# Placing a slot's products with v behind the last quarter of feed-forward products, in a one-core threshold attention and feed-forward kernel

## The chip, the cores and the metric

The kernel runs on one core of one Trainium2 chip. The metric is device microseconds of one launch, the median of several runs. In the profile PE is TensorE (matmul), PEld its weight loads, DVE is VectorE, ACT is ScalarE, POOL is GpSimd and SP is SyncE, which here issues nearly all DMA transfers.

## The reference, cut to what matters

There are 8 batches of 8 heads with 576 tokens and 64 features per head, all in float32. Each score row keeps only what lies within `tau` of its maximum; the attention output, with the heads side by side, is the 576 x 512 input `x` of a feed-forward block with a residual.

```python
scores = scale * np.matmul(q, k.transpose(0, 1, 3, 2))
thresh = np.max(scores, axis=-1, keepdims=True) - tau
scores = np.where(scores >= thresh, scores, -1000000000.0)
attn = np.exp(scores - np.max(scores, axis=-1, keepdims=True))
attn = attn / (np.sum(attn, axis=-1, keepdims=True) + 1e-09)
x = np.matmul(attn, v)                      # then (B, S, H*D)
...
xn = (x - mu) / np.sqrt(var + 1e-06) * g_ln
return x + np.maximum(xn @ w_ch1, 0.0) @ w_ch2
```

## The kernel before, in words

**Slots.** The attention of a batch is cut into 9 slots, s = 0 to 8 (`SLOTS`, L63), so there are 72 slots n = 9b + s (`NS`), all counted from 0. In slots 0 to 3 a pair of heads has its first 256 query rows treated, in slots 5 to 8 its second 256 rows; slot 4 (`s == HP`) takes the last 64 rows of all 8 heads. `scores` (L367) writes a slot's scores into two accumulator tiles, `sc[0]` and `sc[1]`, one for each head of the pair. Each has 1536 columns (three banks of 512): 128 free ones, and then two blocks of 576 columns (L354 to L358). The scores of a head go out in four pieces, and the pieces of both heads are given in turn. The last 256 columns of `sc[0]`, behind its scores, are called `pv_behind` (L356).

**Weights of the attention.** `exponentials` (L390) takes the row maxima (DVE, L398) and the exponentials (ACT, L409). `weights` (L411) masks them with the threshold and sums them (DVE, L416), and takes the reciprocal `den` (L420). The weights must then stand with the keys along the partitions. In batch 0 TensorE turns them, by products with diagonal matrices of `1/den` (`turn_weights`, L443), and ACT copies them out. The diagonals are made on ACT (L427), in batch 0 alone. From batch 1 on (`blocks_go`), POOL divides (L429), DVE transposes 32 x 32 blocks (`turn_blocks`, L494), and the result goes to DRAM and comes back as `em` and `rest` through SP's queue (`fetch`, L505). `em` has one buffer.

**Products with v.** `values_of` (L520) multiplies `v` with the turned weights of the slot before: 20 matmul records for a slot (80 shorter ones for slot s = 4). They go to `pv_behind`, except in batch 0 up to s = 4, where they go to a small tile of the pool `ps_ff`. ACT copies them into `x` (L555; for s = 4 two copies, L546), and POOL adds them to the sum for the mean (L564).

**Feed-forward.** The 576 rows of a batch make two groups of 288 tokens. `ffn_steps` (L632) is a generator over one group: for each of 16 parts of the hidden layer an accumulation `p1` of 4 products, copied out by ACT with a relu (L649), then for each of 4 output parts an accumulation `p2` of 16 products, taken out by DVE (L596). A product is two matmuls, four records (`product`, L95). `p1`, `p2`, `mean`, `var` and the turned weights share two buffers of `ps_ff` (tag `ff`).

**The order.** Every engine gets its instructions in the order in which the program gives them (`manual_schedule`, L136). A slot gives its scores, and then four quarters of feed-forward steps, `second_part(n, 0)` to `second_part(n, 3)` (L702). How many steps a quarter gets follows from fixed shares (`ROOM`, L681) and from when the next group is ready (`ready`, L695). Around the quarters calls are run that were put down for a later slot and quarter with `at_quarter` (L688) by `run(n, i)` (L691). The products with v of slot n are put down for slot n + 1, quarter 3 (quarter 1 in batch 0 up to s = 4). `run(n, 3)` stands ahead of `second_part(n, 3)`, so the order on TensorE is: scores, quarters 0, 1, 2, products with v, quarter 3, scores of the next slot. In the first dozen slots `tick` gives pieces of a conversion of the weights `w_ch1` and `w_ch2` from 64-bit numbers to DVE, ACT and POOL as well.

Of the kernel before, what the change touches and what calls it, by code (L numbers as in the profile page):

```python
# [8 lines left out]
F32 = mybir.dt.float32  # L9
# [9 lines left out]
def kernel(  # L19
# [31 lines left out]
    nc = tc.nc  # L51
# [4 lines left out]
    HP = H // 2  # L56
# [4 lines left out]
    TOK = S // 2  # L61
    QH = 256
    SLOTS = 2 * HP + 1  # L63
    NG = 2 * B
    NS = B * SLOTS
# [8 lines left out]
    ffn = ctx.enter_context(tc.tile_pool(name="ffn", bufs=2))  # L74
# [8 lines left out]
    ident = consts.tile([128, 128], F32, name="ident")  # L83
# [18 lines left out]
    def load_qk(u, engines=(nc.sync, nc.sync), room=None):  # L102


        b, hp = units[u]
        tiles = []
        for i, (name, src) in enumerate((("q", q), ("k", k))):
            if room is None:
                t = ins.tile([128, NB, 32], F32, tag=name, bufs=1, name=f"{name}_in")
            else:  # L110
                t = room[:, i * S : i * S + S].rearrange("p (n c) -> p n c", c=32)
            for h in range(2):
                for e in range(2):
                    g = 2 * h + e
                    engines[i].dma_start(  # L115
                        out=t[32 * g : 32 * g + 32],
                        in_=src[b, 2 * hp + h, :, 32 * e : 32 * e + 32].rearrange(
                            "(n r) c -> r n c", r=32
                        ),
                    )  # L120
            tiles.append(t)
        loaded[u] = tuple(tiles)
# [43 lines left out]
    class Weights:  # L166
# [139 lines left out]
        def tick(self):  # L306
            self.ticks += 1
            if self.ended < self.masked:
                self.end()
            if self.masked < self.carried and self.due[self.masked] <= self.ticks:  # L310
                self.mask()
            if self.carried < self.begun:
                self.carry()
            if self.begun < self.fetched:
                self.begin()
# [51 lines left out]
    def scores(b, s):  # L367


        hp, half = (s, 0) if s < HP else (s - HP - 1, 1)  # L370

        pieces = []
        for h in range(2):
            t = 0
            for j in range(2):
                first = FREE + j * S
                for at, n in span(first, S):
                    pieces.append((t, h, j, at, n, at - first))
                    t += n
        for t, h, j, at, n, o in sorted(pieces):  # L380
            r = slice(64 * h, 64 * h + 64)
            for i in range(2 if s == HP else 1):
                qT, kT, ql = turned[b * HP + (2 * j + i if s == HP else hp)]
                nc.tensor.matmul(  # L384
                    sc[h][64 * i : 64 * i + 64 if s == HP else 128, at : at + n],
                    lhsT=ql[r] if s == HP else qT[r, half, j * 128 : (j + 1) * 128],
                    rhs=kT[r, o : o + n], start=True, stop=True,
                )

    def exponentials():  # L390


        neg = small.tile([128, 4], F32, tag="neg", name="neg")
        thr = small.tile([128, 4], F32, tag="thr", name="thr")
        es = att.tile([128, 4, S], F32, tag="e", name="e")
        for h in range(2):
            i = slice(2 * h, 2 * h + 2)
            nc.vector.tensor_reduce(  # L398
                out=neg[:, i], in_=pairs[h],
                axis=AXL.X, op=ALU.max, negate=True,  # L400
            )
            nc.gpsimd.tensor_scalar(  # L402
                out=thr[:, i], in0=neg[:, i], scalar1=-1.0, scalar2=low_sb,
                op0=ALU.mult, op1=ALU.add,
            )
        for i in range(4):
            if i == 2:
                yield es, thr
            nc.scalar.activation(es[:, i], blocks[i], func=AF.Exp, bias=neg[:, i : i + 1])  # L409

    def weights(es, thr, divide):  # L411


        den = small.tile([128, 4], F32, tag="den", name="den")
        for i in range(4):
            nc.vector.scalar_tensor_tensor(  # L416
                out=es[:, i], in0=blocks[i], scalar=thr[:, i : i + 1], in1=es[:, i],
                op0=ALU.is_ge, op1=ALU.mult, accum_out=den[:, i : i + 1],
            )
        nc.vector.reciprocal(den, den)  # L420
        diags = []
        for i in range(4):
            if not divide:
                if i % 2 == 0:
                    two = ffn.tile([128, TOK], F32, tag="o", bufs=6, name="diag")
                diags.append(two[:, i % 2 * 128 : i % 2 * 128 + 128])
                nc.scalar.mul(diags[i], ident, den[:, i : i + 1])  # L427
                continue
            nc.gpsimd.tensor_scalar(  # L429
                out=es[:, i], in0=es[:, i], scalar1=den[:, i : i + 1], scalar2=1.0,  # L430
                op0=ALU.mult, op1=ALU.mult,
            )
        return diags


# [152 lines left out]
    def run_all(calls):  # L588
        now = calls[:]
        calls.clear()  # L590
        for fn in now:
            fn()
# [86 lines left out]
    QUARTERS = 4  # L679
# [11 lines left out]
    def run(n, i):  # L691
        for fn, args in later_calls.pop((n, i), ()):
            fn(*args)

    def ready(g):  # L695

        if g < 2:
            return (24, 42)[g]
        b, t = divmod(g, 2)
        return QUARTERS * (b * SLOTS + (HP, 2 * HP)[t] + 2) + (2, 4)[t]  # L700

    def second_part(n, i):  # L702

        nonlocal issued, owed
        if not queue:
            return
        at = QUARTERS * n + i
        g = issued // STEPS
        left = sum(ROOM[t % QUARTERS] for t in range(at, ready(g + 1))) if g + 1 < NG else 0
        owed += ((g + 1) * STEPS - issued) * ROOM[i] / left if left > 0 else 8  # L710


        got = 1 if i == 0 else 2
        while queue and (owed >= 0.5 or got == 1 and i in (0, QUARTERS - 1)):
            got = next(queue[0], None)
            if got is None:
                queue.pop(0)
                got = 1
            elif got == 0:
                owed = 0.0  # L720
                break
            else:
                issued += 1
                owed -= 1
# [24 lines left out]
    for n in range(NS):  # L749
        b, s = divmod(n, SLOTS)  # L750
        ticks = (1, 3, 4)[: 2 + n // 3] if n < 6 else range(1, 7)

        def tick(i):
            if i in ticks:
                conversion.tick()

        scores(b, s)
        run(n, -1)
        rest = exponentials()
        es, thr = next(rest)  # L760
        run(n, 0)
        conversion.fetch(2)
        run_all(stores)
        second_part(n, 0)
        next(rest, None)

        u = (n + 1) // SLOTS * HP + (n + 1) % SLOTS
        if (n + 1) % SLOTS < HP and u < len(units):
            turn(u)
            if u + 1 < len(units):  # L770
                load_qk(u + 1)
        run_all(aside)
        tick(1)
        run(n, 1)
        second_part(n, 1)
        tick(2)
        blocks_go = by_blocks(b * HP)
        diags = weights(es, thr, blocks_go)
        run_all(aside)
        run_all(stores)  # L780
        tick(3)
        run(n, 2)
        second_part(n, 2)
        tick(4)
        box = []
        if blocks_go:
            scr = turn_blocks(s, es)
            at_quarter(n + 1, 0, lambda s=s, scr=scr, box=box: box.append(fetch(s, scr)))
        else:
            made = turn_weights(s, es, diags)  # L790
            at_quarter(n + 1, -1, next, made)
            at_quarter(
                n + 1, 0 if s <= HP else -1, lambda made=made, box=box: box.append(next(made))
            )
        at_quarter(
            n + 1, 1 if b == 0 and s <= HP else 3,
            lambda b=b, s=s, box=box: values_of(b, s, box[0]),
        )
        if s in (HP, 2 * HP):
            group_ready(2 * b + (s > HP))  # L800
        run_all(aside)
        conversion.fetch(2)
        tick(5)
        run(n, 3)
        if b == 0 and s < HP - 2:
            load_v(s + 2)
        elif n >= SLOTS - 2 and (n + 2) % SLOTS < HP and n < NS - 2:
            load_v((n + 2) // SLOTS * HP + (n + 2) % SLOTS)
        second_part(n, 3)
        tick(6)  # L810
        run_all(aside)
    while later_calls or queue or aside or stores:
# [36 lines left out]
```

## Time and profile before

| | |
|---|---|
| time before, median of 3 | 1444.91 us (1443.7 to 1446.37) |
| profiled span | 1443.0 us |
| TensorE busy | 1389.0 us (96%) |
| VectorE, ScalarE, GpSimd busy | 60%, 29%, 30% |
| feed-forward matmuls, `p1` and `p2` | 515.2 and 513.7 us |
| scores, a slot's 16 matmul records | about 2.2 us |
| products with v, a slot's 20 matmul records | about 2.4 us |
| copy of these products into x (ACT, L555) | 373 ns |

Busy time of a matmul is from its start to its modelled end; neighbours overlap, so busy sums are no throughput. An idle time is put down to the engine whose release came last. A slot from batch 1 on lasts some 17 to 21 us.

### The profile page before, as it was taken

To read this page: it belongs to the slowest core of one execution; us is meant where nothing else is said; L and a number is where in the kernel's file an instruction comes from. 1 tells how busy PE (TensorE), PEld (TensorE's weight loads), DVE (VectorE), ACT (ScalarE), POOL (GpSimd) and SP (SyncE) were. 2 spreads that over 40 slices of the span, in tenths; PEclk is the share of its full clock that TensorE was granted. 3 is DMA by queue.
4 is the path that set the end of the run, shared out by engine and by line. 5 is a ranking of instruction groups with operands and counts; after the bars stand their busy time and mean duration, and the time that the engine had idled before them with its cause. 6 is when DMAs were issued, how large, how long until landed. Compare 5 with 4: busy or idle time off the path is not lost.

```text
span 1443.0 us, 29649 instructions
## 1 busy us (share of the span) xinstructions
PE 1389.0 (96%) x12168; PEld 859.7 (60%) x12168; DVE 871.8 (60%) x1492; ACT 422.2 (29%) x818; POOL 439.1 (30%) x681
## 2 busy tenths in 40 slices
PE   5879999999999999999999999999999999999998
PEld 3655666655556565655556555565556555565664
DVE  5998857556565666566655565556665566656111
ACT  3887513132221313132221312223132322213020
POOL 2444332333323233232322333232332323222100
PEclk8999999999999999999999999999999999999999
DMA  9622466657845677557855577555775578555301
GB/s 226 168 73 83 90 137 157 172 148 162 176 133 145 148 173 173 145 131 171 183 150 145 146 160 167 140 144 143 176 167 143 136 170 185 139 144 137 79 6 17
DMA packets 466840, 205.12 MB, mean 142 GB/s; under 512 B 275024, under 2 KB 428368, under 8 KB 466704
## 3 DMA queue, kind: packets, MB, share of 16 engines
q1 hardware_dynamic: 461936, 202.64, 58.4%
q8 instruction: 95, 1.56, 0.5%
q10 hardware_dynamic: 4736, 0.59, 0.4%
q14 instruction: 41, 0.34, 0.1%
q0 software_dynamic: 32, 0.00, 0.0%
HBM read 119.41 MB, written 83.76 MB: 141 GB/s over the span
## 4 chain that ended last, share of the span: by engine, by line
PE 85%; DVE 4%; DMA 4%; SPq 3%; ACT 2%; issue 1%; POOL 0%; POOLq 0%; DVEq 0%; ACTq 0%
PE p L100 64%; PE sc L538 10%; PE sc L384 9%; SPq L115 2%; DMA em<-scr 1%; DVE e L416 1%; PE tp L100 1%; DVE neg L398 1%; DMA v_in<-in_v_dram 1%; ACT e L409 1%; DMA rest<-scr 0%; DMA scr<-et 0%; PE mean L100 0%; DVE w L263 0%; SPq L500 0%
## 5 line engine op out<-in xcount | busy, mean ns | idle before, releaser
L100 PE MATMUL p<-xc,w 128*64 128x288 f32 x4096 | 515.2, 407 | 7.4 <-ACT hidden L649 5.9
L100 PE MATMUL p<-hidden,w 128*64 128x288 f32 x4096 | 513.7, 407 | 0.0
L100 PEld LDWEIGHTS p<-xc,w 128*64 128x64 f32 x4096 | 294.9, 137 | 211.9 <-ACT hidden L649 12.6
L100 PEld LDWEIGHTS p<-hidden,w 128*64 128x64 f32 x4096 | 297.9, 137 | 196.5 <-issue 9.3
L398 DVE TENSOR_REDUCE neg<-sc 128x2 f32<-128x1152 f32 x144 | 188.7, 1352 | 252.2 <-PE sc L384 252.2
L409 ACT ACTIVATE e<-sc,neg 128x576 f32<-128x576 f32 x288 | 194.5, 742 | 296.5 <-DVE neg L398 290.1
L429 POOL TENSOR_SCALAR e<-e,den 128x576 f32<-128x576 f32 x252 | 187.9, 763 | 239.6 <-DVE den L420 239.5
L416 DVE SCALAR_TENSOR_TENSOR e<-sc,thr,e 128x576 f32<-128x576 f32 x288 | 219.0, 810 | 23.7 <-ACT e L409 23.7
L494 DVE STREAM_TRANSPOSE et<-e 128x1152 f32<-128x1152 f32 x112 | 153.6, 1375 | 77.3 <-POOL e L429 57.1
L649 ACT ACTIVATE hidden<-p 128x288 f32<-128x288 f32 x256 | 105.7, 413 | 292.0 <-PE p L100 290.6
L384 PE MATMUL sc<-kT,qT 64*128 64x384 f32 (+3 forms) x1024 | 150.6, 425 | 20.0 <-DVE qT L344 10.0
L402 POOL TENSOR_SCALAR thr<-neg,low_sb 128x2 f32<-128x2 f32 x144 | 41.6, 289 | 387.4 <-DVE neg L398 382.5
L384 PEld LDWEIGHTS sc<-kT,qT 64*128 64x128 f32 x1024 | 94.2, 191 | 77.5 <-issue 27.0
L538 PE MATMUL sc<-em,v_in 128*64 128x256 f32 (+1 forms) x1408 | 131.3, 330 | 6.0 <-DMA em<-scr 2.2
L538 PEld LDWEIGHTS sc<-em,v_in 128*64 128x64 f32 x1408 | 86.9, 137 | 45.8 <-DVE et L494 7.0
L555 ACT COPY x<-sc 128x256 f32<-128x256 f32 x60 | 22.4, 373 | 286.4 <-PE sc L538 284.4
L596 DVE TENSOR_TENSOR o<-p,rb 128x288 f32<-128x288 f32 x64 | 28.4, 443 | 127.9 <-PE p L100 127.9
L597 POOL TENSOR_TENSOR o<-o,x 128x288 f32<-128x288 f32 x64 | 51.0, 797 | 115.4 <-DVE o L596 114.0
L564 POOL TENSOR_TENSOR sum<-sum,x 128x256 f32<-128x256 f32 (+1 forms) x64 | 32.8, 512 | 97.6 <-ACT x L555 95.1
L655 POOL TENSOR_TENSOR sq<-sq 128x288 f32<-128x288 f32 x48 | 38.8, 808 | 44.0 <-ACT sq L653 41.5
L538 PE MATMUL sc<-rest,v_rest 128*64 128x256 f32 (+1 forms) x352 | 44.7, 329 | 0.0
L100 PE MATMUL tp<-diag,e 128*64 128x128 f32 x576 | 35.5, 278 | 6.6 <-ACT em L462 5.3
(130 smaller groups left out, 701.2 us busy)
## 6 DMA issues: line engine op xcount, KB each, us to landing
scr<-et SPq DMA_DIRECT2D x252, 288.0 KB, 4.6
em<-scr SPq DMA_DIRECT2D x63, 1024.0 KB, 5.9
out_dram<-ot SPq DMA_DIRECT2D x256, 36.0 KB, 4.4
q_in<-in_q_dram SPq DMA_DIRECT2D x124, 72.0 KB, 3.8
k_in<-in_k_dram SPq DMA_DIRECT2D x120, 72.0 KB, 2.8
v_in<-in_v_dram SPq DMA_DIRECT2D x64, 128.0 KB, 4.4
rest<-scr SPq DMA_DIRECT2D x63, 128.0 KB, 6.0
w<-in_moe_w_ch_dram SPq DMA_DIRECT2D x10, 512.0 KB, 6.0
```

What stands on the lines that cost most here:

```text
L100: nc.tensor.matmul(out[r], lhsT=lhsT[:, r], rhs=rhs, **flags)
L384: nc.tensor.matmul(sc[h][64 * i : 64 * i + 64 if s == HP else 128, at : at + n], lhsT=ql[r] if s == HP else qT[r, half, j * 128 : (j + 1) ...
L398: nc.vector.tensor_reduce(out=neg[:, i], in_=pairs[h], axis=AXL.X, op=ALU.max, negate=True,)
L402: nc.gpsimd.tensor_scalar(out=thr[:, i], in0=neg[:, i], scalar1=-1.0, scalar2=low_sb, op0=ALU.mult, op1=ALU.add,)
L409: nc.scalar.activation(es[:, i], blocks[i], func=AF.Exp, bias=neg[:, i : i + 1])
L416: nc.vector.scalar_tensor_tensor(out=es[:, i], in0=blocks[i], scalar=thr[:, i : i + 1], in1=es[:, i], op0=ALU.is_ge, op1=ALU.mult, accum_o ...
L429: nc.gpsimd.tensor_scalar(out=es[:, i], in0=es[:, i], scalar1=den[:, i : i + 1], scalar2=1.0, op0=ALU.mult, op1=ALU.mult,)
L494: nc.vector.transpose(et[:, :, 64 * h : 64 * h + 64].rearrange("p n (j c) -> p j n c", j=2), es[:, 2 * h : 2 * h + 2].rearrange("p j (n c) ...
L538: nc.tensor.matmul(dst[64 * h : 64 * h + 64], lhsT=vt[:, c, h, :] if c < J else vr[:, h, :], rhs=pick(em[:, c] if c < J else er, hp, h), s ...
L597: nc.gpsimd.tensor_tensor(out=o, in0=o, in1=groups[g][:, m], op=ALU.add)
L649: nc.scalar.activation(hidden[:, d], p1, func=AF.Relu)
L655: nc.gpsimd.tensor_tensor(out=sq[:, 0], in0=sq[:, 0], in1=sq[:, c], op=ALU.add)
```

## The change

The function `weights` no longer makes the diagonals; a function `diagonals` does. Up to s = 4 of batch 0 it is called at once, as before. In slots 5 to 8 it is called behind quarter 2's products, so that on ACT the relu copies of that quarter go ahead of the diagonals.

From batch 1 on (`blocks_go`), the products with v of slot n are put down for a quarter 4 of slot n + 1, which `run(n, QUARTERS)` runs behind `second_part(n, 3)`. The order on TensorE becomes: scores, quarters 0, 1, 2, 3, products with v, scores of the next slot. The purpose is to give the way through DRAM (`turn_blocks`, `fetch`) a quarter's products more time before its data are wanted. This holds for the slots n = 9 to 70; the last slot's products stay in quarter 3.

```diff
-        diags = []
-        for i in range(4):
-            if not divide:
-                if i % 2 == 0:
-                    two = ffn.tile([128, TOK], F32, tag="o", bufs=6, name="diag")
-                diags.append(two[:, i % 2 * 128 : i % 2 * 128 + 128])
-                nc.scalar.mul(diags[i], ident, den[:, i : i + 1])
-                continue
+        for i in range(4 if divide else 0):
             nc.gpsimd.tensor_scalar(
...
+        return den
+
+    def diagonals(den):
+        diags = []
+        for i in range(4):
+            if i % 2 == 0:
+                two = ffn.tile([128, TOK], F32, tag="o", bufs=6, name="diag")
+            diags.append(two[:, i % 2 * 128 : i % 2 * 128 + 128])
+            nc.scalar.mul(diags[i], ident, den[:, i : i + 1])
         return diags
...
-        diags = weights(es, thr, blocks_go)
+        den = weights(es, thr, blocks_go)
+        if n <= HP:
+            diags = diagonals(den)
...
         run(n, 2)
         second_part(n, 2)
+        if HP < n < SLOTS:
+            diags = diagonals(den)
...
         at_quarter(
-            n + 1, 1 if b == 0 and s <= HP else 3,
+            n + 1, QUARTERS if blocks_go and n + 1 < NS else 1 if b == 0 and s <= HP else 3,
             lambda b=b, s=s, box=box: values_of(b, s, box[0]),
         )
...
         second_part(n, 3)
+        run(n, QUARTERS)
         tick(6)
         run_all(aside)
```

## The prediction, made before the result

> **What bounds the kernel now.** I read the page first, parts 1 and 4.
>
> ```profile
> PE 1389.0 (96%) x12168; PEld 859.7 (60%) x12168; DVE 871.8 (60%) x1492; ACT 422.2 (29%) x818; POOL 439.1 (30%) x681
> ...
> PE 85%; DVE 4%; DMA 4%; SPq 3%; ACT 2%; issue 1%; POOL 0%; POOLq 0%; DVEq 0%; ACTq 0%
> ```
>
> TensorE is busy for 96%, and 85% of the chain that ended last is on it. So the time is TensorE's work plus its idle time, and an edit is worth what it adds to or takes from that idle time. Next, the waits of TensorE alone, from 191 us (the start of slot 10) to the end, where the products with v are moved:
>
> ```profile
> PE sc L538 <- DMA em<-scr: 2.2, 3, 1.3
> PE p L100 <- ACT hidden L649: 2.1, 3, 0.7
> PE sc L538 <- DVE sq L624: 1.9, 1, 1.9
> PE sc L538 <- DVE et L494: 1.0, 1, 1.0
> PE sc L538 <- issue: 0.8, 1, 0.8
> PE p L100 <- DVE o L596: 0.7, 1, 0.7
> ```
>
> The columns are the total in us, how often, and the longest. The four rows of L538 are the wait that the change aims at: 5.9 us in 6 of 62 slots. The other rows, 2.8 us, belong to feed-forward products. There is little to win: 8.7 us in all.
>
> Then the timeline of one slot's end (slot 18), which the change rearranges:
>
> ```profile
> 347.73 1.90 PE L538 MATMUL sc<-em,v_in 128*64 128x256 f32 x16
> ...
> 349.46 0.60 PE L538 MATMUL sc<-rest,v_rest 128*64 128x256 f32 x4
> ...
> 349.89 2.60 PE L100 MATMUL p<-hidden,w 128*64 128x288 f32 x20
> 350.11 0.37 ACT L555 COPY x<-sc 128x256 f32<-128x256 f32 x1 [9.81 <-PE sc L538]
> ...
> 352.41 1.81 PEld L384 LDWEIGHTS sc<-kT,qT 64*128 64x128 f32 x16 [0.44 <-issue]
> 352.41 2.21 PE L384 MATMUL sc<-kT,qT 64*128 64x384 f32 x16
> ```
>
> ACT copies the products out of `sc[0]` 0.05 us after their end, while TensorE is at quarter 3; the next scores come 1.9 us after that copy. The reader should ask: what if those scores stood directly behind the products with v? They write the same tile, `sc[0]`. So, last, how finely is this tile guarded? Batch 0, where scores come close behind the masks, shows it:
>
> ```profile
> 71.93 0.81 DVE L416 SCALAR_TENSOR_TENSOR e<-sc,thr,e 128x576 f32<-128x576 f32 x1
> 72.67 0.07 DVE L416 DVE_READ_ACCUMULATOR e<-sc,thr,e 128x1 f32 x1
> ...
> 72.80 0.91 PE L384 MATMUL sc<-kT,qT 64*128 64x384 f32 x2 [0.40 <-DVE e L416]
> ...
> 74.15 0.07 DVE L416 DVE_READ_ACCUMULATOR e<-sc,thr,e 128x1 f32 x1
> ...
> 74.27 2.20 PE L384 MATMUL sc<-kT,qT 64*128 64x384 f32 x14 [0.56 <-DVE e L416]
> ```
>
> The first piece of head 0 (columns 128 to 511 of `sc[0]`) starts only when the second mask, which reads columns 704 to 1279, is done at 72.74; head 1's starts when the fourth is done, at 74.22. Neither column nor bank overlaps, and yet the piece waits: the guard is on the whole tile.
>
> The records of the weight loads say the same about ACT. From slot 8 on, the first load of a slot's scores carries a wait on ACT's semaphore in 62 of 64 slots. It is missing in slots 12 and 21, and these are the slots before which a `p1` of quarter 3 had itself to wait for a relu given behind the copy. In slots 0 to 5, whose products go to another tile, none has it. So the first scores of a slot already wait for the copy L555; in the kernel before it is long done.
>
> **What the Trainium skill says.** "PSUM — Partial Sum Buffer", section "PSUM bank collisions raise a hardware error": TensorE and ScalarE must not touch one bank and quadrant at once, so such pairs have to be ordered. `pv_behind` shares its bank with the last piece of `sc[0]`, so some wait is needed; the trace shows it at the first piece, which is in another bank. The same page, "Engine vs sequencer instructions": matmuls start and complete in program order. The trace agrees: at 72.80 the other head's piece waits behind. "Perfetto Trace Analysis", "Identifying Dependency Chains": find an engine's gaps and then the semaphore waited for; that is how I read the records here.
>
> **The change part by part.**
>
> Products with v last. The same instructions run; two effects follow.
>
> (a) Their data get one more quarter, 5 to 9 steps of four records, each record about 0.124 us (92 in 11.38 us): 2.5 to 4.5 us. The longest wait is 1.9 us, so all six go. A wait also costs the overlap of neighbouring matmuls: one lasts 0.406 us and the next pair would start 0.24 us after its start, so 0.17 us each. Gain: 5.9 + 6 x 0.17 = 6.9 us. `em` is released later, but its transfer is issued 1.6 us or more after the scores start, when the products will have ended.
>
> (b) The copy moves between the products' end and the next scores, and nothing is queued on TensorE that may pass it: quarter 0 stands behind the scores. Worked out on slot 18: the last pair of products starts at 349.67, the next would start 0.215 later, and a change from such matmuls to scores costs some 0.10 more (last feed-forward start 352.07, pair 0.24, scores 352.41): 349.98 without a wait. With it: end 350.05, ACT 0.06 later (0.045 to 0.073 over the slots), copy 0.373, ACT to TensorE 0.05 (a copy of `em` from 167.90, 0.59 long; TensorE at 168.54): 350.54. So 0.55 us for each. Behind s = 4 there are two copies (0.27 each, the second 0.16 after the first): 0.61. Scores follow moved products 61 times (slots 11 to 71), 7 of them behind s = 4: 54 x 0.55 + 7 x 0.61 = 34.0 us. ACT is free then: its last relu of quarter 3 is given 2.2 us earlier. Behind the copy ACT has the exponentials, which wait for the new scores' maxima anyway; POOL's adds are wanted only a quarter or more later.
>
> I bound (b) by 0.45 (copy, with latencies half hidden) and 0.80 (0.49 idle plus the full lost overlap of 0.27): 27 to 49 us.
>
> (c) Quarter 3 directly behind quarter 2: could its accumulations wait for buffers? `p2` accumulations end in quarters 1 and 3 there, not in 2, so DVE, busy with the block transposes, holds none up; a relu takes 0.41 us against 2 us of the accumulation between. Nothing.
>
> Diagonals. They last 1.28 us for four on ACT. In slot 6 TensorE waits 2.76 us at 111.73 for two relus at 111.27, which stand behind the diagonals at 108.39; with these behind them the wait shrinks by 1.3 us. In slot 7 the two relus at 135.52 cost TensorE nothing, in slot 8 quarter 2 has no relu, and in slot 5 no feed-forward runs; there the first turning products want the diagonals a little sooner than they come, at most some 0.3 us. I take a gain of 1.3, and between -0.5 and 2.8.
>
> Sum: 34.0 - 6.9 - 1.3 = 25.8 us more: 1444.9 + 25.8 = 1470.7.
>
> **The rivals.** First, the guard is by bank: then only the last piece of `sc[0]`, 1.6 us behind the first, waits for the copy, which is done 0.5 us after the products; nothing is lost and the gains stay: 1444.9 - 8.2 = 1436.7, faster. For it speaks that a bank is all that has to be guarded; against it speak the start at 72.80 and the place of the waits in the records. I give it 5%. Second, stall and gains are as said, but the copy is regularly held up on ACT, or the first scores behind a stall fill the array anew, so that a slot loses 0.80: 49 - 8 = 41 more, 1486. For it: matmuls behind an idle spell start slower (the first score matmul lasts 0.587 us against 0.482); against it: they do so already behind feed-forward products. 12%. Third, stall and gains cancel, 1444.9: the stall would have to be 0.13 us, less than the copy alone. 2%.
>
> **How the numbers follow.** The forecast has 81%, the rivals 5, 12 and 2%. The range takes the lower bound of the stall with the full gains (27 - 8, 1464, and a little less) and reaches to the second rival's edge: 1462 to 1484; what lies below is the first and third rival, above half of the second. Faster 0.05, within 0.2% 0.02, slower 0.93.
>
> **What would show it.** In the profile of after TensorE's waits get a new row at its top: scores L384 waiting for the copy L555 (ACT `x`), some 54 times about 0.48 us, and L546 7 times, about 29 us of idle in all; the rows of L538 waiting for `em` are gone; TensorE's share falls to some 94 to 95%; at 111 us the wait is near 1.5 us. I am wrong if scores start at once behind the products, if idle time before L384 is under 15 us, or if new waits stand before quarter 3's `p`.

## The result, and the profile after

The changed kernel takes 1470.87 us (median of 6 runs, 1469.79 to 1472.86) against 1444.11 us before in the same session: a ratio of 1.0186, 95% interval 1.0173 to 1.0199. It is slower by 26.8 us; 25.8 were forecast.

In the page of after, parts 1 and 4, TensorE has the same 12168 matmuls, a smaller share of a longer span, and ScalarE's share of the chain that ended last rises from 2% to 4%:

```profile
PE 1392.2 (95%) x12168; PEld 854.9 (58%) x12168; DVE 867.4 (59%) x1492; ACT 421.2 (29%) x818; POOL 437.2 (30%) x681
...
PE 87%; DVE 6%; ACT 4%; issue 1%; DMA 0%; POOL 0%; POOLq 0%; ACTq 0%; DVEq 0%
```

The DMA share of the chain fell from 4% to under half a per cent. What took its place stands in TensorE's waits of after, from 191 us to the end (total, how often, longest, in us):

```profile
PE sc L384 <- ACT x L558: 26.6, 54, 0.6
PE sc L384 <- ACT x L549: 3.7, 7, 0.5
PE p L100 <- ACT hidden L652: 2.1, 3, 0.7
PE p L100 <- DVE o L599: 0.7, 1, 0.7
```

The rows of the products with v (L538 before, L541 now) have vanished, and with them 5.9 us of idle time. Two new rows hold 30.3 us: the scores of 61 slots wait for the copy of the products, 54 times for the one copy (L558, L555 before) and 7 times for the two of slot s = 4 (L549). The last two rows are those of before, to a tenth. The end of slot 18 in after's timeline:

```profile
353.28 1.90 PE L541 MATMUL sc<-em,v_in 128*64 128x256 f32 x16
...
355.00 0.60 PE L541 MATMUL sc<-rest,v_rest 128*64 128x256 f32 x4
355.65 0.37 ACT L558 COPY x<-sc 128x256 f32<-128x256 f32 x1 [12.24 <-PE sc L541]
356.07 1.81 PEld L384 LDWEIGHTS sc<-kT,qT 64*128 64x128 f32 x16 [0.93 <-ACT x L558]
356.08 2.21 PE L384 MATMUL sc<-kT,qT 64*128 64x384 f32 x16 [0.47 <-ACT x L558]
```

Products end at 355.60, the copy runs from 355.65 to 356.02, the scores start at 356.08. Each step follows the one before within 0.06 us, and TensorE has nothing to do beside them. From the start of slot 18's scores to that of slot 19's it is 19.06 us now (337.02 to 356.08) and was 18.51 (333.90 to 352.41).

### The profile page after: what moved, and what is told of

The parts are those of the page before. It is cut to its first block, busy times and chain, and to the rows that moved or that the text cites. A ratio compares the mean times of both kernels' runs of the same rounds, so it can differ in the third digit from the quotient of the medians.

```text
span 1469.6 us, 29637 instructions
## 1 busy us (share of the span) xinstructions
PE 1392.2 (95%) x12168; PEld 854.9 (58%) x12168; DVE 867.4 (59%) x1492; ACT 421.2 (29%) x818; POOL 437.2 (30%) x681
## 4 chain that ended last, share of the span: by engine, by line
PE 87%; DVE 6%; ACT 4%; issue 1%; DMA 0%; POOL 0%; POOLq 0%; ACTq 0%; DVEq 0%
PE p L100 65%; PE sc L384 10%; PE sc L541 10%; ACT x L558 1%; DVE neg L398 1%; DVE e L416 1%; ACT e L409 1%; PE tp L100 1%; DVE w L263 1%; DVE w L290 1%; PE mean L100 0%; PE var L100 0%; DMA et<-in_moe_w_ch_dram 0%; DVE w L267 0%; DVE stage L267 0%
## 5 line engine op out<-in xcount | busy, mean ns | idle before, releaser
L100 PEld LDWEIGHTS p<-xc,w 128*64 128x64 f32 x4096 | 291.2, 137 | 217.2 <-ACT hidden L652 14.2
L541 PE MATMUL sc<-em,v_in 128*64 128x256 f32 (+1 forms) x1408 | 130.7, 329 | 0.0
L558 ACT COPY x<-sc 128x256 f32<-128x256 f32 x60 | 22.3, 372 | 330.0 <-PE sc L541 330.0
L541 PEld LDWEIGHTS sc<-em,v_in 128*64 128x64 f32 x1408 | 85.6, 137 | 38.8 <-issue 0.4
L567 POOL TENSOR_TENSOR sum<-x 128x256 f32<-128x256 f32 (+1 forms) x32 | 16.8, 524 | 145.0 <-ACT x L558 89.0
L541 PE MATMUL sc<-rest,v_rest 128*64 128x256 f32 (+1 forms) x352 | 44.3, 329 | 0.0
```

Of the source, the lines that this page charges most:

```text
L100: nc.tensor.matmul(out[r], lhsT=lhsT[:, r], rhs=rhs, **flags)
L541: nc.tensor.matmul(dst[64 * h : 64 * h + 64], lhsT=vt[:, c, h, :] if c < J else vr[:, h, :], rhs=pick(em[:, c] if c < J else er, hp, h), s ...
L567: nc.gpsimd.tensor_tensor(out=sums[g][:, cols], in0=x[:, 0, cols] if c == 1 else sums[g][:, cols], in1=x[:, c, cols], op=ALU.add,)
```

## The experiments

Times are medians; the kernel before took 1444.73 us beside the first four and 1444.90 us beside the last three.

**The diagonals alone.** Against the changed kernel:

```diff
-            n + 1, QUARTERS if blocks_go and n + 1 < NS else 1 if b == 0 and s <= HP else 3,
+            n + 1, 1 if b == 0 and s <= HP else 3,
```

> The diagonals moved as in the change, the products with v left in quarter 3. My theory: the change's gain from the diagonals is the shorter wait in slot 6 (2.8 to 1.6 us) and a little in slot 6's turning, less 0.6 lost in slot 9: about 1.2 us less than before, 1442.9 us; the waits of L538 for em stay near 6 us. Rival, that ACT's load in batch 0 only shifts the wait to a later slot: 1444.1, no change.

Measured: 1441.32 us, ratio 0.9979 (0.9970 to 0.9988), so faster by 3.0 us, with 1.7 to 4.3 as the interval. In its timeline of slot 6 the two relus now stand ahead of the diagonals:

```profile
109.15 0.72 ACT L652 ACTIVATE hidden<-p 128x288 f32<-128x288 f32 x2
...
109.63 1.68 PE L100 MATMUL p<-xc,w 128*64 128x288 f32 x12 [1.60 <-ACT hidden L652]
109.73 1.30 ACT L435 ACTIVATE diag<-ident,den 128x128 f32<-128x128 f32 x4
```

The wait that was 2.76 us is 1.60. Slot 6 takes 30.86 us instead of 32.44 and slot 7 22.11 instead of 22.30: 1.8 us that the trace can place. The rest of the 3.0 is within the interval. (The trace is also 0.5 us shorter in slots 0 to 2, which the edit doesn't touch: scatter of that size is in it.) The rival, that nothing is won, falls.

**The products alone.** Against the changed kernel:

```diff
-        if n <= HP:
+        if not blocks_go:
             diags = diagonals(den)
...
-        if HP < n < SLOTS:
-            diags = diagonals(den)
```

> The products with v last, the diagonals made at once as before. My theory: the whole loss and the gain of the em waits stay, the 1.2 us of the diagonals go: about 1472.1 us, 61 waits of the scores for the copy, some 30 us. Rival, that the two edits lean on each other: within 1 us of 1470.9 or more than 3 us off.

Measured: 1473.62 us, ratio 1.0199 (1.0185 to 1.0213). Its waits of the scores for the copies are the same to a tenth, 26.6 us in 54 and 3.7 us in 7. The time is 1.5 us over the forecast. It lies 28.9 us above the kernel before, the changed kernel 26.8 above its own; the difference of 2.1 us agrees with what the diagonals gave alone. The times alone would not rule out that the edits lean on each other, but the traces do: the two kernels differ by 1.6 us in slot 6, 0.2 in slot 7 and 0.2 in slot 9, and from slot 10 to 70 no slot differs by more than 0.004 us. The two edits add up; the whole loss is the products'.

**The products two steps ahead of the end.** In `second_part`, against the changed kernel:

```diff
         while queue and (owed >= 0.5 or got == 1 and i in (0, QUARTERS - 1)):
+            if i == QUARTERS - 1 and owed < 2.5:
+                run(n, QUARTERS)
             got = next(queue[0], None)
```

> As the change, but the products with v stand some two feed-forward steps (1 us) ahead of the end of quarter 3, so that these steps run while ACT copies. My theory, the loss is the copy of 0.37 us and two latencies with nothing on TensorE to hide them: scores no longer wait for the copy, most of the em waits (6 us) stay gone, so 1437 to 1440 us, faster than before. Rival, that late products cost in themselves (ACT's or POOL's work pushed into the next slot, more changes between kinds of matmul): 1455 us or more, the waits turning up at other instructions.

Measured: 1438.18 us, ratio 0.9955 (0.9942 to 0.9967): faster than both. Its timeline at the end of slot 18 has two steps (8 records) between the products and the scores:

```profile
348.64 0.60 PE L541 MATMUL sc<-rest,v_rest 128*64 128x256 f32 x4
...
349.07 1.14 PE L100 MATMUL p<-hidden,w 128*64 128x288 f32 x8
349.29 0.37 ACT L558 COPY x<-sc 128x256 f32<-128x256 f32 x1 [11.26 <-PE sc L541]
350.14 0.95 PEld L384 LDWEIGHTS sc<-kT,qT 64*128 64x128 f32 x8 [0.44 <-ACT x L558]
350.14 1.08 PE L384 MATMUL sc<-kT,qT 64*128 64x384 f32 x6
```

The copy is over at 349.66, before the two steps are, and TensorE has no idle time ahead of the scores. (The 0.44 us in the row of the weight loads is not lost: before the change the same row had it, as "issue".) In the whole trace no score waits for a copy. One wait for `em` is left, 1.3 us in slot 48; the waits put it down to DVE (`rb`), but `em` landed at 905.97 and its products began at 906.06. The rival, 1455 us or more, falls: what costs 0.55 us a slot is not that the products are late, but that nothing stands behind them.

**The copy twice.** In `values_of`, against the changed kernel:

```diff
-            nc.scalar.copy(x_of(g)[:, hp, :QH], pv)
+            for _ in range(2 if b else 1):
+                nc.scalar.copy(x_of(g)[:, hp, :QH], pv)
```

> As the change, but from batch 1 on the copy of a slot's products into x (not that of slot s = 4) is given twice, with the same data. My theory: the second copy lies on the path of the next scores, 0.27 to 0.37 us more in each of 54 slots: 15 to 20 us more, 1486 to 1491 us, and the wait for L558 grows from 0.49 to some 0.8 us each. Rival, that the copy only seems to end the wait: 1471 us, since ACT is idle there for some 4 us.

Measured: 1492.76 us, ratio 1.0337 (1.0322 to 1.0353), 21.9 us more than the changed kernel (21.3 when each is taken against its own before). The end of slot 18:

```profile
357.18 0.60 PE L541 MATMUL sc<-rest,v_rest 128*64 128x256 f32 x4
357.83 0.78 ACT L559 COPY x<-sc 128x256 f32<-128x256 f32 x2 [12.23 <-PE sc L541]
358.66 2.21 PE L384 MATMUL sc<-kT,qT 64*128 64x384 f32 x16 [0.88 <-ACT x L559]
```

Two copies take 0.78 us, the second 0.41 more, and the wait grows by the same 0.41. The 54 waits sum to 48.4 us, 21.8 more than with one copy, which is the whole difference in time within the scatter. I had expected the second copy to overlap the first, as the two copies of slot s = 4 do, and so 15 to 20; it doesn't. The records show why: the second copy, which writes the same place, itself waits on the semaphore that the first one raises (end at 358.20, start at 358.23), while the second copy of slot s = 4 carries no wait. The rival falls: what ACT takes longer, the kernel takes longer.

**The products in the other tile.**

```diff
-    pv_behind = sc[0][:, FREE + 2 * S : FREE + 2 * S + QH]
+    pv_behind = sc[1][:, FREE + 2 * S : FREE + 2 * S + QH]
```

> As the change, but the products with v go to the free columns of sc[1] instead of sc[0]. My theory, the guard is on the whole tile: head 0's first piece, which writes sc[0], starts at once behind the products and runs alone while ACT copies; the wait for L558 moves to the second piece, head 1's first. Idle time before L384 falls from 30 to under 8 us; but the pieces of the two heads, which run side by side, are now out of step, so I expect part of the loss to stay: 1450 to 1465 us. Rival, that the wait comes from the shared bank or from the order alone: no change, 1471 us, with the wait still at the first piece.

Measured: 1469.28 us, ratio 1.0164 (1.0148 to 1.0179). The end of slot 18:

```profile
354.98 0.60 PE L541 MATMUL sc<-rest,v_rest 128*64 128x256 f32 x4
355.50 0.29 PEld L384 LDWEIGHTS sc<-kT,qT 64*128 64x128 f32 x2 [0.39 <-issue]
355.51 2.75 PE L384 MATMUL sc<-kT,qT 64*128 64x384 f32 x16
355.62 0.37 ACT L558 COPY x<-sc 128x256 f32<-128x256 f32 x1 [12.71 <-PE sc L541]
356.05 1.80 PEld L384 LDWEIGHTS sc<-kT,qT 64*128 64x128 f32 x14 [0.25 <-ACT x L558]
```

The wait moved as my theory had it, not as the rival had. The first two loads (head 0's first piece, which writes `sc[0]`) start at once, while ACT copies; the third, head 1's first piece, waits for the copy. That piece takes columns 128 to 511 of `sc[1]`, the copy reads columns 1280 to 1535, another bank: the guard follows the tile. The time I had wrong: 1450 to 1465 was expected, and it came out near the rival's 1471. No idle time of TensorE stands ahead of the scores any more, and yet the 16 score matmuls last 2.75 us instead of 2.21. The 0.54 us has moved from between the matmuls to among them. In the changed kernel the first pieces of the two heads start 0.006 us apart and run side by side; here head 0's runs without its partner, which starts 0.541 us later, and the rest of head 0's pieces come only behind that. From slot 12 on every slot is as long as in the changed kernel to within 0.07 us, save 21, 39 and 57: they are 0.48 shorter, since a feed-forward wait for a relu shrank there from 0.7 to 0.2 us. So next to nothing of the stall was won.

**One step and three steps ahead.** As with two, with `owed < 1.5` and `owed < 3.5`.

> As the change, but with about one feed-forward step (0.5 us) of quarter 3 behind the products with v. My theory: one step just about covers the 0.47 to 0.55 us from the products' end to the release, so waits of the scores for the copy shrink to under 0.1 us each: 1437 to 1441 us, like two steps ahead or up to 3 us more. Rival, that the lost time is more than the copy and its latencies (0.8 us a slot): 1450 us or more.

Measured: 1439.56 us, ratio 0.9961 (0.9948 to 0.9973). From slot 10 on no wait of TensorE for a copy or for `em` above 0.12 us is left in its trace. But slot 18 takes 18.57 us instead of 18.51; its scores still start 0.06 us behind the copy's end, so one step is a little short. Most slots are 0.06 to 0.12 us longer than with two steps.

> As the change, but with about three steps (1.5 us) behind the products with v. My theory: no wait for the copy, as with two steps; the data of the products come half a microsecond earlier, so perhaps 1 us of em waits more: 1437 to 1441 us. Rival, that the place of the products matters beyond the two waits: more than 3 us from two steps ahead.

Measured: 1439.54 us, ratio 0.9958 (0.9945 to 0.9970). In its waits after 191 us `em` is back, as expected:

```profile
PE sc L541 <- DMA em<-scr: 2.6, 3, 1.4
```

That the half microsecond less is the cause isn't shown: the three waits are in slots 12, 36 and 57, while the one left with two steps is in slot 48. Which slots wait for `em` differs from trace to trace; in that of the diagonals alone, where the products stand as before, slots 12, 20 and 36 show idle time that they don't show before, and the sum is 6.4 us instead of 5.9. The intervals of one, two and three steps overlap, so which is best is open; each beats both kernels.

## Why the prediction was right, point by point

**The stall (b).** Right in mechanism and size. Slot by slot, the changed kernel and the one with the products two steps ahead differ by 34.1 us over 60 slots (I leave out slot 48, where the latter still waits for `em`); 34.0 us over 61 was forecast. A slot with one copy loses 0.54 to 0.57 us against the forecast's 0.55 (50 of 54; slots 10, 11, 39 and 48 differ in other waits too), one with two copies 0.60 (slot 14: 17.84 us against 17.24). The idle time in the waits was to be about 29 us and is 30.3. Two readings in the prediction don't hold as they stand, without harm to it. The terms of the upper bound, 0.49 and 0.27, make 0.76 us and not 0.80. And head 1's piece waits behind 72.80 for its own masks, so that this alone doesn't show the order on TensorE; what shows it is head 0's second piece, whose tile was free from 72.74 on and which starts at 74.28, just behind head 1's first at 74.27.

**The gain of the data (a).** The six waits are gone, as said. Over slots 10 to 70 the change adds 27.8 us. With 34.6 for the stall in all 61 slots and 1.5 for the next point that leaves a gain of 8.3 us, where 6.9 was forecast. Part of the surplus: a wait turns out to cost some 0.22 us beyond its idle time, not 0.17 (slot 29 waited 1.03 us and is 1.25 shorter with two steps behind the products). Part lies in slots such as 12 and 38, which are 0.2 us shorter in that kernel though the trace before shows no idle time of TensorE in them. The row of the weight loads shows what it was: before the products it stood idle for 0.48 us in slot 12 and 0.43 us in slot 38, where 0.10 is usual, and its loads came 0.10 us behind the landing of `em` (239.88 and 239.98 in slot 12). These are waits for `em` too, covered by the modelled ends of the matmuls before.

**Quarter 3 directly behind quarter 2 (c).** This was costed at nothing and is not quite that. In six slots (16, 34, 43, 52, 61, 70) quarter 2 ends with `var`, one product long, and the next accumulation wants a buffer whose relu began only with `var`. The changed kernel's timeline in slot 16:

```profile
311.96 0.66 PE L100 MATMUL var<-sq,avg_sb 128*64 128x288 f32 x4
312.17 0.41 ACT L652 ACTIVATE hidden<-p 128x288 f32<-128x288 f32 x1 [1.53 <-PE p L100]
312.63 3.59 PEld L100 LDWEIGHTS p<-xc,w 128*64 128x64 f32 x32 [0.53 <-ACT hidden L652]
312.63 4.10 PE L100 MATMUL p<-xc,w 128*64 128x288 f32 x32
```

The same place in the kernel before:

```profile
310.22 0.66 PE L100 MATMUL var<-sq,avg_sb 128*64 128x288 f32 x4
310.70 1.90 PE L538 MATMUL sc<-em,v_in 128*64 128x256 f32 x16
...
312.86 4.05 PE L100 MATMUL p<-xc,w 128*64 128x288 f32 x32
```

After the change the row of the weight loads waits 0.53 us for the relu, while TensorE's own row shows no idle time, since the last matmuls' modelled ends cover it. Before, the products with v stood between `var` and the accumulation and hid it. The kernel with two steps behind the products has these six slots 0.25 us longer than before, 1.5 us in all, while no other slot from 10 to 70 grew by more than 0.01. I had argued from 2 us of accumulation between, and overlooked `var`.

**The diagonals.** Forecast 1.3 us; the trace places 1.8 (slots 6 and 7), the times say 3.0 with 1.7 to 4.3. What I missed is in slot 6's turning, where I feared a loss of 0.3: the wait of `tp` for ACT shrank there from 1.78 to 1.35 us. The changed kernel's trace gives 0.64 back in slot 9, where a piece of the weights' conversion waits for its transfer. This isn't an effect of the change: the kernels with one, two and three steps behind the products and with the copy twice give the same instructions up to there, and their slot 9 takes 26.99 us, as in the kernel before.

**The sum.** The change adds 27.8 us in slots 10 to 70 and takes 1.2 in those before, which makes the 26.6 us between the traces. The forecast's 25.8 came so near partly by luck: it has the gain of the data 1.4 us too small, puts (c) at nothing where it costs 1.5, and is 0.6 us low in the stall and has the gain in slots 6 and 7 0.5 us too small; these errors partly cancel, and the 0.64 us of slot 9 is not the change's.

**The rivals.** A guard by bank would have given 1436.7: the waiting pieces in both placements of the products write another bank than the copy reads, so it falls. A loss of 0.80 us a slot falls by the slot lengths. That stall and gains cancel falls with the time.

## What to carry to other kernels

Before moving work behind another piece of work, ask what the next instruction of that engine waits for: a wait that has been over for 2 us today is free only as long as something stands between. If a transfer needs a later consumer, put the consumer late but not last, and leave as much independent work behind it as the hand-over behind it takes (here two steps of 0.5 us for 0.55; with one, 0.06 us and more of most slots was still lost). And compare the lengths of whole stages, not the idle time alone: loss can hide where an engine counts as busy.

## What the runs showed that I had not expected

Two losses of TensorE showed no idle time of TensorE: 0.54 us a slot where head 0's first score piece ran without its partner (16 matmuls in 2.75 us instead of 2.21), and 0.25 us in six slots behind `var`. The row of the weight loads showed the second, with a wait of 0.53 us, and in the same way some waits for `em` before the change (0.48 us in slot 12). For the first, only the order of the single matmuls tells.
